# Attention into a squared-ReLU MLP: a fixed order on every engine, sums of g spread over the score bursts, x copies on two engines

## The chip, the cores and the metric

The kernel runs on one core of a Trainium2 chip. A core has five engines that run side by side, each through its own list of instructions in order: TensorE (PE, matrix products into PSUM), VectorE (DVE), ScalarE (ACT), GpSimd (POOL), and SyncE (SP), which here only issues DMAs. The metric is the device time of one execution in microseconds (us). A profiled execution gives the trace; its span runs from the first instruction to the last.

## The reference

Eight batches of 12 heads, 448 tokens and 64 dimensions go through an attention without softmax; the heads are then laid side by side and go through a two-layer network with a squared ReLU.

```
scores = scale * q @ k.T                    # per batch and head, 448 x 448, scale = 1/8
attn   = maximum(scores, 0)**2 / 448
x      = (attn @ v), heads side by side     # 3584 x 768
g      = maximum(x @ w_in, 0)**2            # w_in 768 x 2048
out    = g @ w_out                          # w_out 2048 x 768, float32
```

All inputs are float32; the kernel computes in float16 with float32 accumulation.

## The kernel before, in words

**Units and rounds.** A unit is four heads of one batch (NU = 3 units to a batch, 24 in all). q and k of a unit are loaded by SP (`load_qk`), cast to float16 (`cast_qk`, L93, mostly on POOL), and turned: units 1 to 5 on PE (`turn_pe`, L106), later ones by DMA transposes on SP (`turn_dma`, L100). v is loaded by a DMA that POOL issues (`load_v`, L115). A unit has seven rounds; round r covers 64 keys of four heads.

**A round.** `scores` (L377) makes four small matmuls into a two-bank PSUM tile `sp`; there are two such tiles, so a round needs the tile of the round before last to be free. `soft` (L390) turns it into the squared ReLU `at` in one of two ways. `relu2` (L179) squares on ACT (line L180) and then masks by the sign of `sp` on DVE (L181, "the mask"); `sp` is free after the mask. `relu2_wide` (L184) makes a ReLU on ACT into a float32 SBUF tile `rel` (L187; two of these) and multiplies it with itself on POOL (L188); `sp` is free after ACT. When a unit's rounds are done, `av` (L402) multiplies `at` with v over 28 matmuls into two PSUM banks `avt`, and two ACT passes copy these into the tile `xt` (L424).

**The first layer.** `h_groups` (L190): for each of 16 blocks of 128 columns, six matmuls into a bank `hps`, then `relu2` into `g` (ACT L180, DVE L181). One such group takes PE 1.14 us.

**The second layer.** Batch 0 uses `plain_groups`. All others use Strassen-like pairs (`o_groups`, L246): two chunks of 128 rows of g, split in two halves, are multiplied by the four quarters of w_out in seven products instead of eight. A product is eight matmuls (1.30 us). It needs four sums of pieces of g, made on DVE (`combine`, L251 to L253, tile `comb`): s1 = a21 + a22, s2 = s1 - a11, s3 = a11 - a21, s4 = a12 - s2. The products run in the order m1 (a11), m2 (a12), m6 (s2), m5 (s1), m7 (s3), m3 (s4), m4 (a22): the first two and the last need no sum. `part` (L278) copies a bank out on ACT; `close` (L283) adds a copied part to a bank on DVE and stores the result through SP; m2, m7, m3 and m4 end with a close. The combinations of w_out are made once by POOL (`combine_w2`, L141). The last 64 rows of each batch are gathered by POOL (`rest`, L216) and are paired two batches at a time.

**The order of the work.** After a start that streams the first 23 rounds, the loop at L519 goes over bursts of two rounds: both rounds' `scores`, then, if a unit is complete, its `av`, then `soft` for the two, then `push_dense` when a batch is complete, then loads, casts and transposes (`upkeep`), then as much dense work from a queue (`fifo`) as an even share of what is queued. `push_dense` (L338) queues a batch's first-layer groups interleaved with left-over second-layer products, and behind them the batch's own pairs. `chain` (L321) puts the sums of a chain's first pair ahead of its m1 and m2, and the next pair's sums among the products of the pair before. There are seven such chains, one for each batch from 1 to 7, with 2, 1, 3, 1, 2, 1 and 3 pairs; the last one runs after all bursts, as the tail.

**Who decides the order.** L48 fixes the order as written for PE and SP alone. ACT, DVE and POOL are put in order by the compiler's scheduler, which may move an instruction ahead of others written before it. Only the first 23 rounds (inside L464) are fixed on all engines.

Of the kernel before, what the change touches and what calls it, by code (L numbers as in the profile page):

```python
# [11 lines left out]
AF = mybir.ActivationFunctionType  # L12
# [4 lines left out]
def kernel(  # L17
# [27 lines left out]
    CX = 1.0 / 896.0  # L45
    CO = 2.0 ** -42

    ctx.enter_context(tc.manual_schedule(engines={mybir.EngineType.PE, mybir.EngineType.SP}))  # L48

    const_p = ctx.enter_context(tc.tile_pool(name="const", bufs=1))  # L50
    v_p = ctx.enter_context(tc.tile_pool(name="vp", bufs=4))
# [101 lines left out]
    def w2_block(lower, j, cols):  # L153
        return w2[2 * lower + j // 4][:, j % 4, cols]
# [68 lines left out]
    def chunk(b, c):  # L223
        return lambda: gts[b][:, :, c * P:(c + 1) * P], [(b, 2 * c), (b, 2 * c + 1)]
# [21 lines left out]
    def o_groups(one, two):  # L246
        (get1, at1), (get2, at2) = one, two
        lo, hi = slice(0, NH), slice(NH, NF)
        st: dict = {}

        def combine(name, op, x, y):  # L251
            t = comb_p.tile([P, NH, P], FP16, name="comb", tag="comb")
            op(t, x, y)  # L253
            st[name] = t

        def s1():
            a1, a2 = get1(), get2()
            st["a11"], st["a12"], st["a22"] = a1[:, lo], a1[:, hi], a2[:, hi]
            combine("s1", nc.vector.tensor_add, a2[:, lo], a2[:, hi])

        def s2():
            combine("s2", nc.vector.tensor_sub, st["s1"], get1()[:, lo])

        def s3():
            combine("s3", nc.vector.tensor_sub, get1()[:, lo], get2()[:, lo])

        def s4():
            combine("s4", nc.vector.tensor_sub, get1()[:, hi], st["s2"])

        def product(bank, a, w, first, last):  # L270
            if first:
                st[bank] = mm_p.tile([P, 512], FP32, name="ops", tag="mm")
            for j in range(NH):
                nc.tensor.matmul(  # L274
                    st[bank][:, 0:HALF], lhsT=st[a][:, j, :], rhs=w(j),
                    start=(first and j == 0), stop=(j == NH - 1), skip_group_check=True)

        def part(name, bank):  # L278
            st[name] = part_p.tile([P, HALF], FP32, name="part", tag="part")
            nc.scalar.activation(  # L280
                out=st[name], in_=st[bank][:, 0:HALF], func=AF.Copy, scale=CO)

        def close(at, cols, bank, name, sign=1.0):  # L283
            osb = part_p.tile([P, HALF], FP32, name="osb", tag="part")
            nc.vector.scalar_tensor_tensor(  # L285
                out=osb, in0=st[bank][:, 0:HALF], scalar=sign * CO,
                in1=st[name], op0=ALU.mult, op1=ALU.add)
            store(at, cols, osb)

        def m1():  # L290
            product("x", "a11", lambda j: w2_block(0, j, LO), True, True)
            part("r1", "x")

        def m2():
            product("y", "a12", lambda j: w2_block(1, j, LO), True, True)
            close(at1, LO, "y", "r1")

        def m6():
            product("x", "s2", lambda j: t2[:, j, :], False, True)
            part("r2", "x")  # L300

        def m5():
            product("z", "s1", lambda j: t1[:, j, :], True, True)
            part("r5", "z")

        def m7():
            product("x", "s3", lambda j: w2_block(0, j, HI), False, True)
            part("r3", "x")
            close(at2, HI, "x", "r5")

        def m3():
            product("z", "s4", lambda j: w2_block(1, j, HI), False, True)
            close(at1, HI, "z", "r2")

        def m4():
            product("w", "a22", lambda j: t4[:, j, :], True, True)
            close(at2, LO, "w", "r3", -1.0)

        return (s1, s2, s3, s4), [(162.5 * NH, fn) for fn in (m1, m2, m6, m5, m7, m3, m4)]

    def chain(pairs):  # L321

        new = []
        for i, (sums, groups) in enumerate(pairs):
            ahead = pairs[i + 1][0] if i + 1 < len(pairs) else ()
            for k, g in enumerate(groups):
                item = []
                if i == 0 and k < 2:
                    item += [(0.0, fn) for fn in sums[2 * k:2 * k + 2]]
                if 2 <= k < 6 and ahead:  # L330
                    item.append((0.0, ahead[k - 2]))
                new.append(item + [g])
        return new

    QUOTA = (4, 12, 9, 12, 12, 13, 12, 99)
    backlog: list = []
# [1 line left out]
    def push_dense(b):  # L338

        hs = h_groups(b)  # L340
        if b == 0:
            new = [[g] for c in range(2) for g in plain_groups(chunk(b, c))]
        elif b % 2 == 0:
            new = chain([o_groups(chunk(b, 0), chunk(b, 1))])
        else:
            pr = b // 2
            pairs = [o_groups(chunk(b - 1, 2), chunk(b, 0)), o_groups(chunk(b, 1), chunk(b, 2))]
            if pr % 2 == 1:
                pairs.insert(1, o_groups(rest_chunk(pr - 1), rest_chunk(pr)))
            new = chain(pairs)  # L350
        old = backlog[:QUOTA[b]]
        done = 0
        for i, g in enumerate(hs):
            push([g])
            upto = (i + 1) * len(old) // len(hs)
            for z in old[done:upto]:
                push(z)
            done = upto
            if b == 0 and 4 <= i < 16 and i % 2 == 1:
                push([(0.0, lambda k=(i - 4) // 2: combine_w2(k, nc.gpsimd))])  # L360
        if b % 2 == 1:
            push([(0.0, lambda: rest(b // 2))])
        backlog[:] = backlog[len(old):] + new
        now = QUOTA[b] - len(old)
        for z in backlog[:now]:
            push(z)
        del backlog[:now]
        if b == 0:
            push([(0.0, lambda k=k: combine_w2(k, nc.gpsimd)) for k in (6, 7)])
# [32 lines left out]
    def av(n, t):  # L402

        b, u = divmod(n, NU)
        if n == NU * b and t == 0:
            xts[b] = x_p.tile([P, NM, S], FP16, name="xt", tag="xt")
        vs = vst[n]
        if t == 0:
            avs_open[n] = [mm_p.tile([P, 512], FP32, name="avt", tag="mm") for _ in range(2)]
        ap = avs_open[n]  # L410
        at = ats.pop((n, t))
        for e in range(2):
            for c in range(2):
                f = c ^ e
                r = slice(64 * c, 64 * c + 64)
                nc.tensor.matmul(  # L416
                    ap[f][64 * e:64 * e + 64, 0:S],
                    lhsT=vs[r, e ^ c, t * D:(t + 1) * D],
                    rhs=at[r, e, :],
                    start=(t == 0), stop=(t == TJ - 1), skip_group_check=True)  # L420
        if t < TJ - 1:
            return
        for f in range(2):
            nc.scalar.activation(  # L424
                out=xts[b][:, 2 * u + f, :], in_=ap[f][:, 0:S], func=AF.Copy, scale=CX)

    pool, dve, act = nc.gpsimd.tensor_copy, nc.vector.tensor_copy, nc.scalar.copy

# [8 lines left out]
    def av_burst(n):  # L437
        return (TJ * (n + 1) - 1) // 2 + 2
# [4 lines left out]
    def upkeep(i):  # L443

        for n in range(NU, NUN):
            b, u = divmod(n, NU)
            if i == av_burst(n - 1) and NU + 2 < n + 3 < NUN:
                load_v(n + 3)
            if i == max(TJ * n // 2, STREAM // 2):
                if 5 < n + 3 < NUN:  # L450
                    for w in "kq":
                        load_qk(n + 3, w, nc.sync)
            if i == (TJ * n + 4) // 2:
                if n + 2 < NUN:
                    for w in "kq":
                        cast_qk(n + 2, w, pool)
                if n + 1 < NPE:
                    turn_pe(n + 1, "k", dve)
                    turn_pe(n + 1, "q", act)
                if NPE <= n + 2 < NUN:  # L460
                    for w in "kq":
                        turn_dma(n + 2, w)
# [56 lines left out]
    for i in range(STREAM // 2, NB):  # L519
        g = []  # L520
        for r in range(max(STREAM, 2 * i), 2 * i + 2):
            n, t = divmod(r, TJ)
            g.append((n, t, scores(n, t)))
        if i in avs:
            for t in range(TJ):
                av(avs[i], t)
        for z, a in enumerate(g):
            soft(*a, pool=z == 1 and i > av_burst(2 * NU - 1))
        if i in pushes:
            push_dense(pushes[i])  # L530
        upkeep(i)
        nxt = min([j for j in pushes if j > i] or [NB + 2])
        run_some(max(0.0, (queued - KEEP) / (nxt - i)))
# [37 lines left out]
```

## Time and profile before

| | us |
|---|---|
| median of 2 runs (408.81 and 411.44) | 410.12 |
| the profiled execution | 412.48 |
| its span | 410.6 |
| PE busy | 380.4 |
| DVE busy | 269.2 |
| ACT busy | 259.6 |
| POOL busy | 216.6 |
| PE, mean granted clock | 0.972 of full speed |

Rows that the steps use, each with its count, busy time and mean: score masks on DVE (128x896) 98, 105.4 us, 1088 ns; g masks on DVE (128x448) 128, 79.3 us, 624 ns; closes on DVE 52, 28.4 us, 552 ns; sums on DVE (128x1024, float16) 52 in all, 48.4 us, the shortest 675 ns and the longest 2168 ns; POOL's multiplies 62, 104.2 us, 1685 ns; POOL's w_out combinations 8, 24.7 us, about 3.1 us each; x copies on ACT 48, 23.9 us.

How to read a line of the timeline: start in us from the span's start, duration, engine, source line, operation, output and inputs, shapes, a count where like neighbours are merged, and in brackets how long the engine was idle before it and which instruction ended that. PE's weight loads (PEld) are a row of their own. A matmul's duration holds its pipeline's end, so the start of the next one, not the end of the last, tells when PE was free.

### The profile page before, as it was taken

What the parts mean: (1) busy time and instruction counts of PE and PEld (TensorE: products, weight loads), DVE (VectorE), ACT (ScalarE), POOL (GpSimd) and SP (SyncE); (2) the same over time, 40 slices, a digit from 0 to 9 for tenths busy, and PEclk for the clock granted to TensorE, in tenths of its full rate; (3) what the DMA queues carried; (4) which work ended last, traced back from release to release, by engine and by line L of the source; (5) the groups of instructions that cost most, each with busy time, mean ns of one, the idle gap of its engine ahead of it and who ended that gap; (6) DMA issues with size and microseconds to landing.
All of it is one profiled execution on the core that took longest, in us unless ns stands there. A gap on an engine that the chain in (4) does not pass through costs nothing.

```text
span 410.6 us, 7636 instructions
## 1 busy us (share of the span) xinstructions
PE 380.4 (93%) x3000; PEld 190.4 (46%) x3000; DVE 269.2 (66%) x347; ACT 259.6 (63%) x407; POOL 216.6 (53%) x186
## 2 busy tenths in 40 slices
PE   6757999798999999999999999999979999999995
PEld 2323454344445445444454454444434445555562
DVE  2977898634784667676897565965694566456741
ACT  3787787656865877777666676677654776244111
POOL 5851778669666568467846664754743335101000
PEclk9885999999999999999999999999998999999998
DMA  8999996878138945596388654575514000220243
GB/s 251 300 251 242 227 219 136 152 163 234 22 60 225 192 84 116 145 208 128 44 214 175 132 149 114 113 167 130 90 39 104 21 19 21 48 50 0 59 97 77
DMA packets 67619, 53.58 MB, mean 130 GB/s; under 512 B 36864, under 2 KB 67584, under 8 KB 67584
## 3 DMA queue, kind: packets, MB, share of 16 engines
q1 hardware_dynamic: 55152, 40.84, 39.0%
q0 software_dynamic: 12160, 11.80, 19.1%
q8 instruction: 23, 0.38, 0.4%
q10 hardware_dynamic: 272, 0.46, 0.3%
q14 instruction: 12, 0.10, 0.1%
HBM read 45.61 MB, written 11.01 MB: 138 GB/s over the span
## 4 chain that ended last, share of the span: by engine, by line
PE 74%; DVE 9%; ACT 7%; DMA 3%; issue 3%; POOL 2%; SPq 1%; ACTq 0%; DVEq 0%; POOLq 0%
PE hps L198 33%; PE ops L274 24%; PE sp L384 8%; PE avt L416 7%; DVE comb L253 4%; DVE at L181 3%; ACT at L180 2%; ACT rel L187 2%; DMA qf<-in_q_dram 2%; POOL w L151 2%; DVE g L181 1%; PE ops L236 1%; ACT g L180 1%; DMA kf<-in_k_dram 1%; PE tps L110 1%
## 5 line engine op out<-in xcount | busy, mean ns | idle before, releaser
L198 PE MATMUL hps<-xt,w 128*128 128x448 f16 x768 | 157.4, 356 | 1.0 <-ACT xt L424 0.6
L188 POOL TENSOR_TENSOR at<-rel 128x896 f16<-128x896 f32 x62 | 104.2, 1685 | 72.2 <-ACT rel L187 72.1
L181 DVE SCALAR_TENSOR_TENSOR at<-sp,at 128x896 f16<-128x896 f32 x98 | 105.4, 1088 | 32.9 <-ACT at L180 32.6
L181 DVE SCALAR_TENSOR_TENSOR g<-hps,g 128x448 f16<-128x448 f32 x128 | 79.3, 624 | 65.5 <-ACT g L180 65.5
L198 PEld LDWEIGHTS <-w 128*128 128x128 f16 x768 | 72.5, 98 | 77.5 <-issue 16.7
L180 ACT ACTIVATE g<-hps 128x448 f16<-128x448 f32 x128 | 69.9, 548 | 55.3 <-PE hps L198 54.5
L180 ACT ACTIVATE at<-sp 128x896 f16<-128x896 f32 x98 | 88.3, 916 | 19.7 <-PE sp L384 19.6
L384 PE MATMUL sp<-qT,kT 64*64 64x448 f16 x672 | 54.3, 376 | 18.6 <-DVE at L181 11.4
L187 ACT ACTIVATE rel<-sp 128x896 f32<-128x896 f32 x70 | 64.7, 924 | 6.8 <-PE sp L384 3.6
L280 ACT ACTIVATE part<-ops 128x384 f32<-128x384 f32 x52 | 25.6, 493 | 47.5 <-PE ops L274 45.8
L274 PEld LDWEIGHTS <-comb 128*128 128x128 f16 x416 | 39.0, 98 | 34.6 <-DVE comb L253 5.1
L285 DVE SCALAR_TENSOR_TENSOR osb<-ops,part 128x384 f32<-128x384 f32 x52 | 28.4, 552 | 29.5 <-ACT part L280 17.7
L416 PE MATMUL avt<-at,vs 64*64 64x448 f16 x672 | 44.1, 370 | 1.5 <-DVE g L181 1.0
L384 PEld LDWEIGHTS <-kT 64*64 64x64 f16 x672 | 16.8, 106 | 52.3 <-issue 49.4
L274 PE MATMUL ops<-wt,comb 128*128 128x384 f16 x208 | 36.5, 327 | 2.7 <-DVE comb L253 2.7
L96 POOL CAST ks<-kf 128x896 f16<-128x896 f32 x21 | 20.3, 967 | 34.1 <-DMA kf<-in_k_dram 26.1
L274 PE MATMUL ops<-w,comb 128*128 128x384 f16 x208 | 36.8, 326 | 0.0
L274 PEld LDWEIGHTS <-g 128*128 128x128 f16 x264 | 25.2, 99 | 20.3 <-issue 4.4
L121 POOL DMA_DIRECT2D vs<-in_v_dram x48 | 29.8, 628 | 9.0 <-PE sp L384 5.9
L274 PE MATMUL ops<-w,g 128*128 128x384 f16 x176 | 30.9, 326 | 0.0
L416 PEld LDWEIGHTS <-vs 64*64 64x64 f16 x672 | 22.3, 111 | 13.4 <-issue 3.5
L219 POOL COPY rest<-g 128x1024 f16<-128x1024 f16 x8 | 10.4, 1295 | 29.8 <-DVE g L181 29.8
(43 smaller groups left out, 217.1 us busy)
## 6 DMA issues: line engine op xcount, KB each, us to landing
out_dram<-osb SPq DMA_DIRECT2D x112, 96.0 KB, 2.2
kf<-in_k_dram SPq DMA_DIRECT2D x22, 448.0 KB, 4.5
qf<-in_q_dram SPq DMA_DIRECT2D x21, 448.0 KB, 5.0
vs<-in_v_dram POOLq DMA_DIRECT2D x48, 112.0 KB, 3.3
w<-in_moe_w_in_dram POOLq DMA_DIRECT2D x4, 768.0 KB, 20.5
w<-in_moe_w_out_dram POOLq DMA_DIRECT2D x4, 768.0 KB, 19.5
early<-in_k_dram SPq DMA_DIRECT2D x2, 448.0 KB, 7.9
early<-in_q_dram SPq DMA_DIRECT2D x2, 448.0 KB, 9.3
```

The source lines that it names most:

```text
L96: op(t.rearrange("p t (f d) -> p f t d", f=2), src.rearrange("p f (t d) -> p f t d", d=D))
L121: nc.gpsimd.dma_start(out=t[64 * r:64 * r + 64], in_=src[:, u, hs])
L180: nc.scalar.activation(out=dst, in_=ps, func=AF.Square, scale=scale)
L181: nc.vector.scalar_tensor_tensor(out=dst, in0=ps, scalar=0.0, in1=dst, op0=ALU.is_gt, op1=ALU.mult)
L187: nc.scalar.activation(out=r, in_=ps, func=AF.Relu, scale=scale)
L188: eng.tensor_mul(dst, r, r)
L198: nc.tensor.matmul(hps[:, 0:S], lhsT=w1[f // 4][:, m, (f % 4) * P:(f % 4 + 1) * P], rhs=xt[:, m, :], start=(m == 0), stop=(m == NM - 1))
L274: nc.tensor.matmul(st[bank][:, 0:HALF], lhsT=st[a][:, j, :], rhs=w(j), start=(first and j == 0), stop=(j == NH - 1), skip_group_check=True)
L280: nc.scalar.activation(out=st[name], in_=st[bank][:, 0:HALF], func=AF.Copy, scale=CO)
L285: nc.vector.scalar_tensor_tensor(out=osb, in0=st[bank][:, 0:HALF], scalar=sign * CO, in1=st[name], op0=ALU.mult, op1=ALU.add)
L384: nc.tensor.matmul(sp[64 * c:64 * c + 64, e, 0:S].rearrange("p (t c) -> p t c", t=TJ), lhsT=kT[r, t, 64 * e:64 * e + 64], rhs=qT[r, :, 64 ...
L416: nc.tensor.matmul(ap[f][64 * e:64 * e + 64, 0:S], lhsT=vs[r, e ^ c, t * D:(t + 1) * D], rhs=at[r, e, :], start=(t == 0), stop=(t == TJ - ...
```

## The change

- `tc.manual_schedule()` without a list of engines: ACT, DVE and POOL also run in the order in which the kernel is written.
- The sums of a chain no longer stand at fixed places in the queue. They go into a list, `sums`, when the queue reaches a marker (`ready`) behind the batch's first layer. Each burst takes one of the list (`sum_one`) just ahead of its masks; a product that needs more sums than have been made takes the missing ones from the list right ahead of itself.
- Of the two x copies of a unit, from unit 3 on, the second is made by DVE.
- Within a burst `soft` is written ahead of `av`; up to burst 22, every odd burst's second round also goes through `relu2_wide` on POOL.
- `load_v` is issued one burst later.

```diff
-    ctx.enter_context(tc.manual_schedule(engines={mybir.EngineType.PE, mybir.EngineType.SP}))
+    ctx.enter_context(tc.manual_schedule())
...
         def s1():
-            a1, a2 = get1(), get2()
-            st["a11"], st["a12"], st["a22"] = a1[:, lo], a1[:, hi], a2[:, hi]
-            combine("s1", nc.vector.tensor_add, a2[:, lo], a2[:, hi])
+            combine("s1", nc.vector.tensor_add, get2()[:, lo], get2()[:, hi])
...
         def m1():
+            st["a11"], st["a12"], st["a22"] = get1()[:, lo], get1()[:, hi], get2()[:, hi]
...
+    sums: deque = deque()
+    made = used = due = 0
+
+    def sum_one():
+        nonlocal made
+        sums.popleft()()
+        made += 1
+
     def chain(pairs):
 
+        nonlocal due
         new = []
-        for i, (sums, groups) in enumerate(pairs):
-            ahead = pairs[i + 1][0] if i + 1 < len(pairs) else ()
-            for k, g in enumerate(groups):
-                item = []
-                if i == 0 and k < 2:
-                    item += [(0.0, fn) for fn in sums[2 * k:2 * k + 2]]
-                if 2 <= k < 6 and ahead:
-                    item.append((0.0, ahead[k - 2]))
-                new.append(item + [g])
-        return new
+        for _, groups in pairs:
+            for k, (c, fn) in enumerate(groups):
+                def item(k=k, fn=fn, need=due + (0, 0, 2, 2, 3, 4, 4)[k]):
+                    nonlocal used
+                    while made < need:
+                        sum_one()
+                    fn()
+                    used += 2 <= k < 6
+                new.append([(c, item)])
+            due += 4
+        return new, lambda: sums.extend(fn for four, _ in pairs for fn in four)
...
         if b % 2 == 1:
             push([(0.0, lambda: rest(b // 2))])
+        if ready:
+            push([(0.0, ready)])
...
-        for f in range(2):
+        nc.scalar.activation(
+            out=xts[b][:, 2 * u, :], in_=ap[0][:, 0:S], func=AF.Copy, scale=CX)
+        if n < NU:
             nc.scalar.activation(
-                out=xts[b][:, 2 * u + f, :], in_=ap[f][:, 0:S], func=AF.Copy, scale=CX)
+                out=xts[b][:, 2 * u + 1, :], in_=ap[1][:, 0:S], func=AF.Copy, scale=CX)
+        else:
+            nc.vector.tensor_scalar_mul(xts[b][:, 2 * u + 1, :], ap[1][:, 0:S], CX)
...
-            if i == av_burst(n - 1) and NU + 2 < n + 3 < NUN:
+            if i == av_burst(n - 1) + 1 and NU + 2 < n + 3 < NUN:
                 load_v(n + 3)
...
+        if sums and made - used < 6:
+            sum_one()
+        for z, a in enumerate(g):
+            soft(*a, pool=z == 1 and (i > av_burst(2 * NU - 1) or i % 2 == 1))
         if i in avs:
             for t in range(TJ):
                 av(avs[i], t)
-        for z, a in enumerate(g):
-            soft(*a, pool=z == 1 and i > av_burst(2 * NU - 1))
```

More of the change, by code (lines that the diff above doesn't have):

```diff
@@ L340, in push_dense @@
         hs = h_groups(b)
+        ready = None
         if b == 0:
@@ L343, in push_dense @@
         elif b % 2 == 0:
-            new = chain([o_groups(chunk(b, 0), chunk(b, 1))])
+            new, ready = chain([o_groups(chunk(b, 0), chunk(b, 1))])
         else:
@@ L349, in push_dense @@
                 pairs.insert(1, o_groups(rest_chunk(pr - 1), rest_chunk(pr)))
-            new = chain(pairs)
+            new, ready = chain(pairs)
         old = backlog[:QUOTA[b]]
```

## The prediction

> **What bounds the kernel now.** First the page's chain of work that ended last, then what TensorE (PE) waited for, then its timeline.
>
> ```profile
> PE 74%; DVE 9%; ACT 7%; DMA 3%; issue 3%; POOL 2%; SPq 1%; ACTq 0%; DVEq 0%; POOLq 0%
> ```
>
> PE carries the end. The page has it busy 380.4 of 410.6 us, and the table by stage 39.8 of 40 us between 130 and 170, so a PE stall adds to the end one for one. After the start (38 us) its timeline shows only these gaps: 0.36, 0.33, 1.83, 0.61, 0.45, 1.52 and 0.37 up to 99 us; then at starts of output chains 0.64 (117), 0.16 (165), 0.64 (203), 2.7 (303 to 308), 0.36 (351), 0.86 (381); and 1.65 around 275. Sum 12.5 us: no change of the other engines can gain much more. PE's waits say the same, most of the first two lying before 38 us:
>
> ```profile
> PE sp L384 <- DVE at L181: 11.4, 11, 2.1
> PE sp L384 <- ACT rel L187: 6.1, 6, 1.6
> PE ops L274 <- DVE comb L253: 2.7, 5, 0.9
> ```
>
> Then the first output chain, all engines by time (start, us, instruction):
>
> ```profile
> 113.40 2.76 PE L274 MATMUL ops<-w,g 128*128 128x384 f16 x16
> 114.83 0.69 DVE L253 TENSOR_TENSOR comb<-g 128x1024 f16<-128x1024 f16 x1
> 115.56 1.69 DVE L253 TENSOR_TENSOR comb<-comb,g 128x1024 f16<-128x1024 f16 x1
> 116.09 0.57 PE L384 MATMUL sp<-qT,kT 64*64 64x448 f16 x8
> 116.53 0.92 ACT L180 ACTIVATE at<-sp 128x896 f16<-128x896 f32 x1 [1.14 <-PE sp L384]
> 117.31 2.77 PE L274 MATMUL ops<-wt,comb 128*128 128x384 f16 x16 [0.64 <-DVE comb L253]
> 118.34 1.68 POOL L188 TENSOR_TENSOR at<-rel 128x896 f16<-128x896 f32 x1 [1.65 <-ACT rel L187]
> ```
>
> m1 and m2 (16 matmuls, 2.6 us) need no sum; meanwhile VectorE (DVE) makes s1 and s2, and m6, which needs s2, starts 0.64 late. This cover of 2.6 us is what I follow through the change.
>
> **What the Trainium skill says.** "SBUF — State Buffer", "Who interferes with whom": a DVE instruction with two SBUF inputs contends with a GpSimd (POOL) instruction that reads SBUF, and the second waits out the first. The trace agrees: alone a sum takes 0.68 us, but
>
> ```profile
> 299.51 1.76 POOL L188 TENSOR_TENSOR at<-rel 128x896 f16<-128x896 f32 x1 [0.93 <-ACT rel L187]
> 299.66 2.16 DVE L253 TENSOR_TENSOR comb<-g,comb 128x1024 f16<-128x1024 f16 x1
> 304.36 1.79 POOL L188 TENSOR_TENSOR at<-rel 128x896 f16<-128x896 f32 x1 [3.09 <-ACT rel L187]
> 304.53 2.17 DVE L253 TENSOR_TENSOR comb<-g 128x1024 f16<-128x1024 f16 x1
> ```
>
> both sums end 0.55 us after POOL's multiply (301.27, 306.15). "TensorE: Matmul & The Clock Gate", "What's actually happening": PE falls to half clock after an idle window of 3413 ns. The trace shows it harsher: the 2.08 us stall before 308.35 was enough (duration, then PE busy; the column after POOL is the granted clock):
>
> ```profile
> 305.60:309.00 3.40, 1.32 (x23) 0.64 (x24) 3.40 (x5) 1.07 (x2) 0.55 (x1) 1.00 0.00 0
> 309.00:312.40 3.40, 3.40 (x29) 1.56 (x22) 1.23 (x2) 1.74 (x3) 1.68 (x1) 0.50 0.38 92
> ```
>
> In those 3.4 us an av burst of 1.43 us took 2.38 and a product of 1.31 took 2.02, a loss of 1.65. The stall of 1.52 us at 97 cost no clock. "TensorE", "Architectural detail", has ACT, DVE and POOL as strict FIFOs: an instruction that waits holds all behind it.
>
> **The change, part by part.** Comparing issue orders, PE's and SyncE's (SP's) are the same in both kernels, SP's transfers included; ScalarE's (ACT's) differs only by the moved work. DVE and POOL differ.
>
> *Sums.* Before, s1 to s4 come right behind the last g mask. In the new order the first chain on DVE reads: g mask, close of m2, s1, score mask, s2, s3, score mask, close of m7, s4, close of m3. A close must wait for its product on PE, so s1 comes after m2, s4 after m7: the cover is gone. I count from t, PE's start of a score burst; its next slot is t+0.50 (120.01 to 120.51).
>
> - *s2 behind the mask (first, second, third chain).* ACT starts at t+0.44 (116.53), the mask 0.95 later (141.14 to 142.09), the next DVE instruction 1.00 after that: t+2.39. POOL's multiply starts 1.81 after ACT (118.34), t+2.25, just ahead, and takes 1.68: t+3.93. So s2 ends at t+4.48 (+0.55), m6 starts at t+4.53 (+0.05): stall 4.03. If DVE got in first, 2.6. I take 4.03.
> - *s4 behind the close of m7.* In chains 1, 3 and 5 m7 follows the burst, ends at t+1.80, the close runs, and s4 again meets POOL: m3 at t+4.53, stall 2.73. In chain 2 an av burst lies between and POOL is done: close starts 0.20 after the product (396.50 against 396.30), s4 0.47 later, 0.68 long, 0.05: 1.40.
> - *s1 and s2 both behind the close of m2 (chains 4, 6, 7):* 0.20 + 0.47 + 0.73 + 0.69 + 0.05 = 2.14.
> - *Chain 5:* close of m2, s2, with POOL's casts in the way: 1.8.
> - *Chain 6 too:* s3 sits behind the new x copy on DVE: 0.2 + 0.62 + 0.68 = 1.5; then s4, 1.40.
> - *Chain 7, the tail, three pairs, no bursts:* each 2.14 + 1.40 = 3.54, so 10.6.
>
> Today's start of the last chain, for contrast, has m6 0.86 late and then no gap to the end:
>
> ```profile
> 377.07 2.76 PE L274 MATMUL ops<-w,g 128*128 128x384 f16 x16
> 380.69 2.77 PE L274 MATMUL ops<-wt,comb 128*128 128x384 f16 x16 [0.86 <-DVE comb L253]
> ```
>
> Later pairs of chains 1, 3 and 5 get their sums a burst ahead: no stall. Sum: 6.8 + 5.4 + 6.8 + 2.1 + 4.5 + 5.0 + 10.6 = 41.2. The same places lose 6.0 today (slot to start: 0.7 + 0.2 + 0.7 + 0 + 2.85 + 0.5 + 1.0). Net +35.2.
>
> *Five score rounds (27, 31, 35, 39, 43) moved from DVE to POOL.* Their buffers are freed by ACT alone, which removes the gaps 0.36, 0.33 and 0.61: -1.3. The 1.83 gap stays: round 44 waits for round 42's mask. POOL gains 5 x 1.69 = 8.4 us of multiplies, and its w2 work (8 x 3.1 us) now alternates with them. By sums of POOL's rows it reaches round 39 at 75.4, before the av burst at 78 that reads it; the w2 pair (6.2) then stands ahead of round 49's multiply, which frees the buffer that ACT needs for round 53: ready at 100.4, PE stalls some 2.2 where it stalls 1.9 now. Net -1.0; with POOL later than summed, up to +5.
>
> *x copies.* 21 copies at 0.50 leave ACT; on DVE a 448-wide PSUM pass takes 0.62 (the g mask). Each starts behind the score mask, at t+2.39, and ends at t+3.0, against 3.15 for ACT's second copy: PE waited 0.63 in total for x, so nothing, both ways, except in chain 6 above.
>
> *POOL's other moves.* v loads (628 ns each) go a burst later, casts of q and k return to their written place, 5 bursts (some 17 us) ahead of use. SP's transposes wait for them, and stores and loads queue behind; the transpose needs 1.25 to 3.6, so this is covered, and costs only where POOL is over 10 us late.
>
> *Clock.* Threshold between 1.52 and 2.08 of idle per window, say 1.75. A stall of 4.03 always leaves one such window: 1.5 each, 3 times. One of 2.73 does with chance 0.77, one of 2.14 with 0.6 (share of window phases), at about 1.5 to 1.6: 3.5 for three, 4.8 for five; 0.5 for chain 5's. Together 13.3, less today's 1.65: +11.6; bounds 0 and 22.
>
> Sum: 35.2 - 1.0 + 11.6 = +46 on the profiled span 410.6 (its execution 412.48; the runs' median is 410.12, so the sum carries over): **456 us**.
>
> **Rivals.**
> 1. *Stalls, no clock loss* (PE's load averaged over longer): 410 + 34 = 444. For: one single event supports the price. Against: that event was the shorter stall.
> 2. *POOL's new order becomes the bound at 43 to 100 us* and delays av bursts, over and above: +5 to +10, 464. For: POOL is busy 41.6 of 57 us there already. Against: the sums leave 2 to 3 us.
> 3. *DVE gets the port first, sums overlap more than counted*: 410 + 20 to 30, 435. For: 0.14 us decide s2. Against: s4 meets POOL well inside.
> 4. *Not slower:* the sum fills DVE's idle 0.9 us ahead of the mask, as in the later pairs. If in every chain s2 and s4 were done before m6 and m3 are due, the 6.0 of chain gaps, 1.65 of clock and 1.0 would go: 401. It decides at t+0.50, where m6 is due. Against: the order puts the close of m2 ahead of s1, and nothing but a score burst or need itself starts a sum; the tail has no bursts.
>
> **How the numbers follow.** Main case 0.5, rival 1 0.2, rival 2 0.13, rival 3 0.1, rival 4 0.07 (faster by over 2% 0.03, within 2% 0.04). Two per cent, 8 us, is about what a measurement here can tell from none. Slower 0.93. The range takes in rivals 1 and 2 and the upper part of 3: 438 to 468.
>
> **What would show it.** In the new profile: PE waiting for comb at L253 some 30 to 40 us in total; in the tail, three pairs with gaps near 2.1 and 1.4; sums of 2.2 us behind score masks; clock 0.5 after the 4 us stalls; the gaps at 50 and 64 us gone. Wrong if s1 starts before m2's close, or if the PE gaps at m6 stay under 1 us.

## The result, and the profile after

The median of two runs is 463.9 us (461.16 to 466.64) against 410.1 for the kernel before: a ratio of 1.131, 95% interval 1.099 to 1.164. The two runs lie 5.5 us apart, so a difference against 463.9 is good to some 3 us. The profiled span is 464.5 us against 410.6. PE is busy 396.0 us (380.4 before), idle 68.5 (30.2), and its mean granted clock is 0.937 (0.972). So of 53.9 us, 38.3 are idle time and 15.6 are longer matmuls.

First the page's chain of work that ended last, then PE's waits (engine and what it ran, releaser: us in total, times, longest):

```profile
PE 69%; DVE 11%; ACT 8%; issue 5%; POOL 4%; DMA 1%; SPq 1%; ACTq 0%; DVEq 0%; POOLq 0%
```

```profile
PE ops L272 <- DVE comb L253: 47.4, 19, 6.0
...
PE sp L396 <- DVE at L181: 5.7, 8, 1.6
```

Waits for sums (L253) rose from 2.7 us in 5 places to 47.4 in 19; waits for masks fell from 11.4 to 5.7. Now the timeline of the first chain (all engines):

```profile
115.00 0.57 PE L396 MATMUL sp<-qT,kT 64*64 64x448 f16 x8
115.18 0.56 DVE L283 SCALAR_TENSOR_TENSOR osb<-ops,part 128x384 f32<-128x384 f32 x1 [1.47 <-PE ops L272]
...
115.65 0.68 DVE L253 TENSOR_TENSOR comb<-g 128x1024 f16<-128x1024 f16 x1
...
116.39 1.09 DVE L181 SCALAR_TENSOR_TENSOR at<-sp,at 128x896 f16<-128x896 f32 x1
117.24 1.68 POOL L188 TENSOR_TENSOR at<-rel 128x896 f16<-128x896 f32 x1 [1.92 <-ACT rel L187]
117.39 2.07 DVE L253 TENSOR_TENSOR comb<-comb,g 128x1024 f16<-128x1024 f16 x1
...
119.53 4.21 PE L272 MATMUL ops<-wt,comb 128*128 128x384 f16 x16 [3.95 <-DVE comb L253]
```

DVE stands still for 1.47 us because the close of m2 (115.18) is at its head. Behind it come s1, the mask, and s2, which loses to POOL by 0.15 us and ends 0.54 after POOL's multiply. m6 starts 3.95 late, and its 16 matmuls then take 4.21 us instead of 2.77. The granted clock (us, duration, then busy time of each engine; the column after POOL is the clock) shows why:

```profile
119.00:122.40 3.40, 2.87 (x10) 1.36 (x11) 3.40 (x2) 0.10 (x1) 2.92 (x4) 0.51 0.56 77
122.40:125.80 3.40, 3.25 (x24) 1.47 (x22) 0.76 (x2) 2.42 (x5) 0.00 (x0) 0.99 0.93 144
```

Chain 5, where the prediction had 1.8 us:

```profile
328.03 0.96 POOL L96 CAST ks<-kf 128x896 f16<-128x896 f32 x1
...
328.90 0.96 POOL L96 CAST qs<-qf 128x896 f16<-128x896 f32 x1
328.96 5.06 DVE L253 TENSOR_TENSOR comb<-comb,g 128x1024 f16<-128x1024 f16 x1
...
329.78 2.04 POOL L219 COPY rest<-g 128x1024 f16<-128x1024 f16 x2
...
331.77 1.69 POOL L188 TENSOR_TENSOR at<-rel 128x896 f16<-128x896 f32 x1
...
334.07 4.46 PE L272 MATMUL ops<-wt,comb 128*128 128x384 f16 x16 [6.05 <-DVE comb L253]
```

s2 takes 5.06 us instead of 0.68: it ends 0.56 after POOL's whole run of casts, copies and a multiply (333.46). And the tail, PE alone:

```profile
423.14 2.77 PE L272 MATMUL ops<-wt,comb 128*128 128x384 f16 x16 [2.03 <-DVE comb L253]
...
428.99 1.47 PE L272 MATMUL ops<-w,comb 128*128 128x384 f16 x8 [1.77 <-DVE comb L253]
```

The same 2.03 and 1.77 stand before m6 and m3 of all three pairs, where the kernel before lost 0.86 once.

### The profile page after: what moved, and what is told of

Same layout as the page of the kernel before. It is cut to its first block, busy times and chain, and to the rows that moved or that the text cites. A ratio compares the mean times of both kernels' runs of the same rounds, so it can differ in the third digit from the quotient of the medians.

```text
span 464.5 us, 7617 instructions
## 1 busy us (share of the span) xinstructions
PE 396.0 (85%) x3000; PEld 194.2 (42%) x3000; DVE 283.0 (61%) x363; ACT 250.1 (54%) x386; POOL 223.4 (48%) x191
## 4 chain that ended last, share of the span: by engine, by line
PE 69%; DVE 11%; ACT 8%; issue 5%; POOL 4%; DMA 1%; SPq 1%; ACTq 0%; DVEq 0%; POOLq 0%
PE hps L198 27%; PE ops L272 25%; PE sp L396 7%; PE avt L428 6%; DVE comb L253 5%; DVE at L181 3%; ACT at L180 3%; ACT rel L187 2%; ACT part L278 1%; DVE osb L283 1%; PE ops L236 1%; PE warm L495 1%; POOL w L151 1%; POOL at L188 1%; DMA qf<-in_q_dram 1%
## 5 line engine op out<-in xcount | busy, mean ns | idle before, releaser
L188 POOL TENSOR_TENSOR at<-rel 128x896 f16<-128x896 f32 x67 | 112.4, 1678 | 148.1 <-ACT rel L187 148.0
L181 DVE SCALAR_TENSOR_TENSOR at<-sp,at 128x896 f16<-128x896 f32 x93 | 100.5, 1089 | 49.8 <-ACT at L180 49.3
L180 ACT ACTIVATE at<-sp 128x896 f16<-128x896 f32 x93 | 84.1, 915 | 32.5 <-PE sp L396 32.4
L272 PEld LDWEIGHTS <-comb 128*128 128x128 f16 x416 | 40.8, 104 | 88.0 <-DVE comb L253 55.3
L187 ACT ACTIVATE rel<-sp 128x896 f32<-128x896 f32 x75 | 69.3, 924 | 5.1 <-POOL at L188 2.9
L272 PE MATMUL ops<-wt,comb 128*128 128x384 f16 x208 | 44.7, 376 | 28.1 <-DVE comb L253 28.1
L396 PE MATMUL sp<-qT,kT 64*64 64x448 f16 x672 | 56.0, 391 | 13.4 <-ACT rel L187 6.6
L272 PE MATMUL ops<-w,comb 128*128 128x384 f16 x208 | 38.5, 329 | 19.4 <-DVE comb L253 19.4
L219 POOL COPY rest<-g 128x1024 f16<-128x1024 f16 x8 | 8.1, 1040 | 33.8 <-DVE g L181 33.8
L253 DVE TENSOR_TENSOR comb<-g 128x1024 f16<-128x1024 f16 x22 | 22.2, 1009 | 0.0
```

Source lines behind the costliest of these rows:

```text
L180: nc.scalar.activation(out=dst, in_=ps, func=AF.Square, scale=scale)
L181: nc.vector.scalar_tensor_tensor(out=dst, in0=ps, scalar=0.0, in1=dst, op0=ALU.is_gt, op1=ALU.mult)
L187: nc.scalar.activation(out=r, in_=ps, func=AF.Relu, scale=scale)
L188: eng.tensor_mul(dst, r, r)
L272: nc.tensor.matmul(st[bank][:, 0:HALF], lhsT=st[a][:, j, :], rhs=w(j), start=(first and j == 0), stop=(j == NH - 1), skip_group_check=True)
L396: nc.tensor.matmul(sp[64 * c:64 * c + 64, e, 0:S].rearrange("p (t c) -> p t c", t=TJ), lhsT=kT[r, t, 64 * e:64 * e + 64], rhs=qT[r, :, 64 ...
```

## The experiments

My theory after the result: the sums are late since, in a fixed order, they stand behind closes and masks. The rivals: that one half of the change alone, the fixed order or the new place of the sums, does it. All ratios are to the kernel before, measured on the same chip in the same batch, with 95% intervals.

| label | us | ratio |
|---|---|---|
| b_fixed | 447.5 | 1.091 (1.088 to 1.093) |
| b_newsums | 410.5 | 1.002 (1.000 to 1.003) |
| a_sched | 423.0 | 1.034 (1.031 to 1.037) |
| a_m6 | 424.8 | 1.035 (1.031 to 1.038) |
| a_m3 | 455.2 | 1.108 (1.104 to 1.112) |
| a_both | 416.1 | 1.014 (1.012 to 1.017) |
| a_fill | 453.8 | 1.107 (1.103 to 1.111) |
| a_both_rest | 418.1 | 1.019 (1.015 to 1.023) |
| a_both_run | 414.0 | 1.009 (1.006 to 1.013) |
| a_best | 408.3 | 0.996 (0.994 to 0.997) |
| a_best_x | 406.7 | 0.993 (0.991 to 0.995) |
| a_best_mask | 409.5 | 1.000 (0.999 to 1.002) |

**One half of the change at a time.** b_fixed is the kernel before with this edit only:

```diff
-    ctx.enter_context(tc.manual_schedule(engines={mybir.EngineType.PE, mybir.EngineType.SP}))
+    ctx.enter_context(tc.manual_schedule())
```

> The kernel before with the fixed order on all engines and nothing else changed; its sums stay at their written places ahead of m1 and m2. Theory (the loss comes from sums placed behind the closes and masks, not from a fixed order): within 2% of 410, say 408 to 416. Rival (a fixed order by itself costs tens of microseconds, through POOL's and DVE's waits in line): 425 or more.

Measured: 447.5. My expectation missed by far. The timeline of its first chain:

```profile
118.24 6.57 DVE L253 TENSOR_TENSOR comb<-comb,g 128x1024 f16<-128x1024 f16 x1
...
118.83 2.04 POOL L219 COPY rest<-g 128x1024 f16<-128x1024 f16 x2
120.82 1.70 POOL L188 TENSOR_TENSOR at<-rel 128x896 f16<-128x896 f32 x1
...
123.32 0.94 POOL L96 CAST qs<-qf 128x896 f16<-128x896 f32 x1
...
124.87 2.42 PE L274 MATMUL ops<-wt,comb 128*128 128x384 f16 x7 [7.27 <-DVE comb L253]
```

Here the sums are written ahead of m1 and m2, and still s2 ends at 124.81, 0.55 after POOL's last cast. PE waits for sums 23.6 us in seven places (7.27 twice); in the tail, where POOL rests, it waits 0.86, as before. The rest of the 37 us is mostly longer waits for masks (16.3 us against 11.4) and 10.0 us of longer matmuls. So the old written order is bad under a fixed order for another reason than the new one, and this trace points to POOL's unbroken runs, which hold s2 in both places of 7.27; under the scheduler no sum took over 2.17 us.

b_newsums is the other half: the list of sums (`s1` to `s4`, `chain`, `push_dense` and the burst's `sum_one` as in the diff of the change), the scheduler and all else as before.

> The kernel before with only the sums taken over from the change (the list, one per burst, the rest at the product that needs them); the scheduler still orders VectorE, ScalarE and POOL, and x copies and score rounds are as before. Theory (the written place of the sums costs time whoever orders the engines, since the scheduler moves them ahead only in part): 425 to 450. Rival (the loss needs the fixed order, the scheduler hoists the sums as soon as g is there): 408 to 415.

Measured: 410.5; the rival was right. PE waits for sums 2.5 us in four places. The timeline shows what the scheduler did:

```profile
113.37 0.69 DVE L253 TENSOR_TENSOR comb<-g 128x1024 f16<-128x1024 f16 x1
...
114.09 1.69 DVE L253 TENSOR_TENSOR comb<-comb,g 128x1024 f16<-128x1024 f16 x1
...
115.84 2.45 PE L272 MATMUL ops<-wt,comb 128*128 128x384 f16 x14 [0.64 <-DVE comb L253]
```

s1 and s2 (and s3 at 115.71) run right behind the last g mask and ahead of the close of m2, as in the kernel before, though they are written elsewhere. The place of the sums alone costs nothing.

a_sched takes the changed kernel and gives back only its first edit:

```diff
-    ctx.enter_context(tc.manual_schedule())
+    ctx.enter_context(tc.manual_schedule(engines={mybir.EngineType.PE, mybir.EngineType.SP}))
```

> The changed kernel with its first edit alone undone: ACT, DVE and POOL go back to the compiler's scheduler; the list of sums, the x copies, the rounds on POOL, soft ahead of av and the later v loads stay. Theory (the loss needs both halves: a fixed order, and sums written behind closes): the scheduler puts s1 to s3 right behind the last g mask, so the waits at L272 for comb fall from 47 us to under 5 and no half clock is left in the chains: 409 us (406 to 413), a ratio of 0.99 to 1.007. Rival (the moved masks and x copies or POOL's rounds cost by themselves, hidden so far among the stalls): 415 to 425.

Measured: 423.0. The waits for sums fell as forecast (2.5 us in four places), the time did not. It lies in the rival's range, and it went to one of POOL's new rounds, but through the scheduler's order and not through stalls that had been hidden. In its timeline:

```profile
61.73 3.08 POOL L147 TENSOR_TENSOR wt<-w,wt 128x1536 f16<-128x1536 f16 x1 [0.29 <-DMA w<-in_moe_w_out_dram]
64.77 1.68 POOL L188 TENSOR_TENSOR at<-rel 128x896 f16<-128x896 f32 x1
...
66.50 0.59 PE L428 MATMUL avt<-at,vs 64*64 64x448 f16 x4 [12.40 <-POOL at L188]
```

The scheduler put two casts and two of POOL's w_out combinations, which wait for weights to land, ahead of the multiply of one of the five new POOL rounds, whose input was ready at 54.10; the av burst waited 12.40 us for it, and the clock was at half from 59.3 to 69.5. In the changed kernel PE has no wait for POOL. So with the five rounds on POOL the scheduler's order is no way back: that part of the change leans on the fixed order, and the sums, as they are written in it, lean on the scheduler.

**Where in the chains the time is lost.** Three kernels change only the table of sums that a product asks for:

```diff
-                def item(k=k, fn=fn, need=due + (0, 0, 2, 2, 3, 4, 4)[k]):
+                def item(k=k, fn=fn, need=due + (2, 2, 2, 2, 3, 4, 4)[k]):
```

This is a_m6: s1 and s2 are written ahead of m1. a_m3 has (0, 0, 2, 2, 4, 4, 4): s4 ahead of m7. a_both has (2, 2, 2, 2, 4, 4, 4).

> The changed kernel with one tuple changed: a pair's first two sums are taken at its m1 instead of at its m6, so s1 and s2 stand ahead of the closes of m1 and m2. Theory: the nine stalls at m6 (3.95 three times, 6.05, 2.03 five times, 28 in all) shrink to those of the kernel before (some 3) and about six of the nine half-clock windows go with them: 464 - 25 - 8 = 431 (425 to 438). Rival (no clock loss of its own, windows come by chance): 439. Rival (the sums are late for another reason, such as POOL holding the port): over 450.

> The changed kernel with one tuple changed: the fourth sum is taken at m7 instead of at m3, so s4 stands ahead of the close of m7. Theory: the stalls at m3 (2.60 three times, 1.77 five times, 16.6 in all) go, with three half-clock windows: 464 - 16 - 4 = 444 (438 to 450). Rival (s4 still meets POOL's multiply): stalls of some 1.3 us stay in the three chains with bursts, 450.

> The changed kernel with both tuple changes: two sums at m1, the fourth at m7. Theory: all comb stalls but some 4 us go, and the clock windows with them: 409 (404 to 415). If something besides the place of the sums costs time (the x copies on DVE, POOL's added multiplies, the fixed order), it stays above 418.

Measured: 424.8, 455.2 and 416.1; all three lie outside the expected ranges, by 0.2, 5 and 1 us. The gains against 463.9 are 39.1 and 8.7 us apart and 47.8 together, so they add, within the 3 us that this figure is good for. a_m6 gained more than expected: all stalls ahead of m6 but chain 5's are down to 0.9 us or less, and those ahead of m3 in chains 1, 2, 3 and 5 too, since the bursts now make s3 and s4 instead of s1 and s2. a_m3 gained less: it removes the 1.77 in chain 6 and the tail and shortens chain 2's to 1.27, but where a burst lies between (chains 1, 3, 5) 2.60 stays, since s4 still meets POOL's multiply. In a_both, chain 5's stall is left: 6.04 us at 304.26, with 6.8 us of half clock.

**The clock by itself.** a_fill puts 20, 32 or 11 matmuls without use into a free bank ahead of m6, sized to each stall, so that PE is busy while it waits:

```diff
+        def m6(fill=0):
+            if fill:
+                st["z"] = mm_p.tile([P, 512], FP32, name="ops", tag="mm")
+                for j in range(fill):
+                    nc.tensor.matmul(
+                        st["z"][:, 0:HALF], lhsT=ident, rhs=w2_block(0, 0, LO),
+                        start=True, stop=True, skip_group_check=True)
```

> The changed kernel with idle matmuls (identity by a block of w_out, into the bank that m5 is about to overwrite) right ahead of each m6: 20 in chains 1, 2 and 3 (3.3 us), 32 in chain 5 (5.2), 11 elsewhere (1.8), each shorter than the stall it stands in. The results are unchanged. Theory (stalls drop the granted clock, and that costs beside the stall itself): the half-clock windows behind m6 go, the stalls stay as long; m6 and m5 after them take 2.6 instead of 4.2 to 4.5, 464 - 10 = 454 (450 to 457). Rival (the clock drops whatever TensorE does in the stall, or the fillers delay m6): 462 to 468.

Measured: 453.8, as expected. The timeline of chain 1:

```profile
114.12 3.42 PE L301 MATMUL ops<-w,ident 128*128 128x384 f16 x20
...
116.01 2.08 DVE L253 TENSOR_TENSOR comb<-comb,g 128x1024 f16<-128x1024 f16 x1
...
118.14 1.15 PE L272 MATMUL ops<-wt,comb 128*128 128x384 f16 x6 [0.60 <-DVE comb L253]
```

s2 takes 2.08 us, as in the changed kernel (2.07), and m6 starts 4.53 us behind the burst in both (113.61 to 118.14 here, 115.00 to 119.53 there), but the 16 matmuls of m6 and m5 take 2.77 us. The half-clock spells of the chains, eight in the changed kernel, are down to one (at 222.6, behind a stall of 2.60 ahead of m3), and 10.1 of the 53.8 us are gone (7.4 and 12.9 against the two runs of the changed kernel). After the first 46 us the matmuls without the fillers take 346.9 us, against 360.8 in the changed kernel and 347.1 in the kernel before. No sum came earlier, so this is the price of the clock, not of the wait.

Which stall costs the clock can be read from the traces. In each of them all half-clock spells start on one grid of 3.41 us, which lies at another offset in each run. Two stalls of the same 2.03 us in the changed kernel, each with its window of the grid and the next (PE's busy time stands behind the duration, the clock behind POOL):

```profile
433.10:436.51 3.41, 1.38 (x9) 0.67 (x8) 2.02 (x4) 0.49 (x1) 0.00 (x0) 1.00 0.40 94
436.51:439.92 3.41, 3.41 (x12) 1.62 (x11) 0.43 (x1) 0.49 (x1) 0.00 (x0) 0.50 0.16 37
385.31:388.72 3.41, 1.44 (x9) 0.67 (x7) 1.84 (x3) 0.49 (x1) 0.73 (x1) 1.00 0.29 69
388.72:392.13 3.41, 3.35 (x32) 1.91 (x36) 0.01 (x1) 0.98 (x2) 0.00 (x0) 1.00 0.20 46
```

The first stall lies in one window, in which PE is idle for 2.03 us; the second reaches into the next one and leaves 1.97. In the fourteen profiles (both kernels and the twelve of the table), after the first 46 us, 1471 windows began at full clock. All 32 with 2.02 us or more of idle PE were followed by half clock, and none of the 1439 with 2.00 or less. In the first 46 us the limit lies lower, near 1.65.

**POOL's run in chain 5.** a_both_rest is a_both with the copies of `rest` queued behind the fifth product of each chain; a_both_run is that with chain 5's casts on ACT:

```diff
-        if b % 2 == 1:
-            push([(0.0, lambda: rest(b // 2))])
...
-        for z in backlog[:now]:
+        for k, z in enumerate(backlog[:now]):
             push(z)
+            if b % 2 == 1 and k == 4:
+                push([(0.0, lambda: rest(b // 2))])
...
-                        cast_qk(n + 2, w, pool)
+                        cast_qk(n + 2, w, act if n == 20 else pool)
```

> The kernel a_both (two sums at m1, the fourth at m7) with POOL's two gathers of the last rows put behind the chain's fifth product. Theory (a sum on VectorE has to wait for the end of POOL's whole unbroken run of work, not of one instruction): chain 5's stall of 6.04 shrinks by the two gathers, 2.0, to about 4.0, time 414. Rival (a sum waits for one POOL instruction only; the 6.04 is something else): no change, 416.

> As a_both_rest, and the two casts of q and k at chain 5 go to ScalarE, so that POOL has only the v loads and one multiply there. Theory (unbroken run): s2 comes after that multiply, stall 2.6 or less, and the double half-clock window behind it goes: 410 (407 to 413). Rival as for a_both_rest: 416.

Measured: 418.1 and 414.0. In chain 5 both did what they should: s2 took 6.57 us in a_both, 4.61 without the copies in POOL's run, and 0.69 without the casts too, and m6 was 6.04, 4.08 and 0.17 late:

```profile
302.49 1.24 POOL L121 DMA_DIRECT2D vs<-in_v_dram  x2
...
303.12 0.69 DVE L253 TENSOR_TENSOR comb<-comb,g 128x1024 f16<-128x1024 f16 x1
...
303.87 2.77 PE L272 MATMUL ops<-wt,comb 128*128 128x384 f16 x16 [0.17 <-DVE comb L253]
```

The times missed, because in chains 1 and 3 the moved copies got in the way of another sum. In chain 1 they lengthened a run of POOL, and the sum took 5.70 us; in chain 3 the sum reads the copied rows, started 2.16 us late and took 2.16. The mask behind it on DVE came late, and a score burst stalled 2.45 us in each.

**A version without these stalls, and two parts priced on it.** a_best has the copies of `rest` late in chain 5 alone:

```diff
-        if b % 2 == 1:
+        if b % 2 == 1 and b != 5:
             push([(0.0, lambda: rest(b // 2))])
...
+            if b == 5 and k == 4:
+                push([(0.0, lambda: rest(b // 2))])
```

a_best_x is a_best with both x copies on ACT (`n < NUN` instead of `n < NU`); a_best_mask is a_best without the five early POOL rounds (`pool=z == 1 and i > av_burst(2 * NU - 1)`).

> The changed kernel with the needs (2, 2, 2, 2, 4, 4, 4), chain 5's casts on ACT and the rest copies behind the fifth product in chain 5 alone, at their first place in chains 1, 3 and 7. Theory: against the version with rest copies late everywhere (414.0) the two stalls of 2.45 us in chains 1 and 3 go, and the half clock behind one of them (1.7): 407.5 us (405 to 410), slightly below the kernel before. Rival (POOL's run at its first place blocks the sums in chains 1 and 3 just as long once the casts are elsewhere, or another half clock comes): 412 to 416.

> The same as the version with rest late in chain 5 alone, and both x copies of a unit on ACT as before the change. Theory of the prediction (the copy on DVE ends about when ACT's second did, so it is worth nothing but at one place in chain 6): within 1 us of that version, either way. Rival (ACT's second copy delays the first group of the next layer, at the 21 units): 2 to 6 us longer. Rival 2 (DVE's copy delays masks or sums): 1 to 3 us shorter.

> The same as the version with rest late in chain 5 alone, without the five score rounds moved to POOL up to burst 22. Theory of the prediction: the three gaps at 50, 64 and near 90 us come back (0.36, 0.33 and 0.61): 1.3 us longer (0.5 to 2.5). Rival (POOL's w2 work, no longer delayed, lets later rounds on time): 1 to 3 us shorter.

Measured: 408.3, 406.7 and 409.5. a_best came out as expected: the two stalls of 2.45 us are gone and PE waits for sums 3.6 us in all, against 2.7 in the kernel before. a_best_x is 1.6 us faster than a_best by the medians, as rival 2 had it: DVE's x copy had held s3 of chain 6, and its stall of 1.32 us is missing from a_best_x's trace (2.3 us of waits for sums). a_best_mask is 1.3 us slower, the number expected, but not by the gaps expected: that of 0.37 at 50 us stands in both. What comes back is 1.83 and 0.62 us at 77 and 78 where a_best has one of 1.51, with one half-clock window behind them. a_best_x beats the kernel before by 0.7% (0.5% to 0.9%): a small gain, a third of the 2 per cent that the prediction took as about what can be told from none.

## Why the prediction was right

It gave 456 us and a range of 438 to 468; 463.9 lies in it, and the waits that make up most of it came where and as forecast. One term was right in size by luck alone (the five rounds on POOL). The first step held: a waiting instruction held those behind it (DVE's 1.47 us behind the close at 115.18). Step by step, on the profiled spans (+53.9 against +46):

- *s2 behind the mask*: 4.03 forecast, 3.95 measured in all three chains. The order in which the mask, POOL's multiply and the sum started was as counted. Of rival 3 (DVE first) nothing was seen there.
- *s4 behind the close of m7*: 2.73 forecast, 2.60 measured (chains 1, 3, 5). Where POOL was quiet 1.40 was forecast and 1.77 measured in five places. The close started 0.04 us behind the end of ACT's `part` of the same bank (427.74 and 427.78 in the tail), not 0.20 behind the product: this wait for the other reader was missing in my sum, 5 x 0.37 = 1.9 us. The trace before had it: there the close of m7 starts 0.03 behind ACT's `part` (394.44 and 394.47); the 0.20 came from a close without such a `part`.
- *s1 and s2 behind the close of m2*: 2.14 forecast, 2.03 measured, in all five places. Chain 6's s3: 1.5 and 1.32.
- *Chain 5* is the term that was mis-sized: 1.8 forecast, 6.05 measured. The prediction named POOL's casts as in the way and not the copies and the multiply behind them; s2 waited for all of them. a_both_rest and a_both_run, which shorten the run piece by piece, shorten the sum with it (6.57, 4.61, 0.69 us).
- *"Later pairs of chains 1, 3 and 5 get their sums a burst ahead: no stall"*: right but for one place. At 248.60 m3 of chain 3's second pair started 1.39 late: its s4 stood behind g masks.
- *Sum of the stalls*: 41.2 forecast, 47.4 measured, above the 30 to 40 named as a sign; some 4 of the 6.2 more are chain 5's.
- *Five rounds on POOL and POOL's order*: -1.0 forecast; the gaps over 0.3 us between 38 and 110 us went from 5.47 to 3.72. The size is luck, for the step was wrong: the gaps at 50 and 64 us were to go, and they stand at 54.01 and 68.51, 0.37 each. PE waits there for the second of two masks that DVE runs in a row (51.87 and 66.37), so the buffer is still freed by a mask on DVE. What shrank is 1.83 and 0.61, now one gap of 1.51, and 1.52, now 1.02, where 2.2 was forecast; the 0.37 at 99 is gone. By a_best_mask the rounds are worth 1.3 us. That they lean on the fixed order (a_sched) I had not seen.
- *x copies*: nothing but in chain 6, as a_best_x shows.
- *Clock*: +11.6 forecast, PE's busy time grew by 15.6. Some 1.9 of this lies in the first 46 us (33.26 and 35.15 busy), where the half-clock spells differ from run to run: 27.3 us of them in the changed kernel, 13.7 in a_m6, whose start is the same. That leaves 13.7. Of rival 1 (no clock loss) a_fill disposes: 10.1 us came back when PE was kept busy. The idea of idle time per window was right and the threshold taken, 1.75 us, too low: the windows above put it at 2.0. Of the stalls of 2.03 the changed kernel lost the clock after one of five and a_m3 after three of five, where 0.6 of them were forecast; of those of 2.60 the changed kernel in all three places, a_m3 and a_fill in one of three each, where 0.77 were forecast.

Rival 2 (POOL the bound between 43 and 100 us) gave 464, but the gaps there shrank: its figure is met by another way. Rival 4 failed as a forecast, but its mechanism is what the later runs built: once the sums stand ahead of the closes and clear of POOL's runs, the loss is gone (a_best, 408.3).

What stays open: by what rule the port is handed over when POOL has several instructions in a row, for a sum often gets in behind the first of them (last section); and why the limit of the clock lies lower in the first 46 us.

## What to carry to other kernels

A scheduler's freedom can be worth more than any edit it stands beside: before fixing an engine's order, list for each instruction that feeds the critical engine what is written ahead of it and what that waits for. Here the fixed order alone cost 37 us, the moved sums alone nothing, and both together, with the rest of the change, 54. In a fixed order, write an operand of the critical engine ahead of everything that waits for this same engine, and keep two-input sums on VectorE away from runs of GpSimd work, not only from single instructions.

## What the runs showed of the hardware that was not expected

- *A two-input sum on VectorE can wait for a whole run of GpSimd instructions.* "SBUF — State Buffer", "Who interferes with whom", of the Trainium skill says that who issues first gets the shared port pair for the whole instruction, and the other blocks. These traces show more: with casts, copies and a multiply back to back on POOL, a sum that alone takes 0.68 us ended 0.55 us after the last of them, after 5.06 us (changed kernel) and 6.57 us (b_fixed, a_both). While POOL only issued the DMAs of v, with no reading instruction behind them, a sum took 0.69 (a_both_run, 303.12). Nor does each run hold a sum to its end: over the fourteen profiles 18 sums waited for two to five such instructions in a row, and 65 waited for the one under way alone, as in a_best, where a sum at 110.82 took 1.14 us and ended 0.55 behind the first of two copies, while the second took 1.50 us instead of 1.03.
- *The clock falls after stalls shorter than the window of 3413 ns* that the skill states in "TensorE: Matmul & The Clock Gate", "What's actually happening": past the first 46 us, after each window of 3.41 us with 2.02 us or more of idle PE, 32 in fourteen profiles, and after none of the 1439 with 2.00 or less. So the same stall costs the clock or not by where it lies on the grid: in the changed kernel in all four places of 3.95 us and more, in all three of 2.60, in one of five of 2.03. Matmuls without use in the stall kept it up.
- *A close that reads a bank which ScalarE is still copying out starts when that copy ends* (0.04 us behind it in the tail, 0.03 in the kernel before at 394.47): two readers of one bank did not overlap there. The trace shows it as a wait for ScalarE; what imposes that wait was not tested.
